# Turned spectrum copied from PSUM in runs of 8 by another grouping of the inverse rows; two W columns fetched over 128 partitions by the software queue; four A1 buffers

## Chip, cores, metric

One core of one Trainium2 chip. The metric is the device time of one execution in microseconds (us). The kernel before takes 497 us (median of its first three runs 496.99, from 496.23 to 497.87).

Names: PE is TensorE (PEld its weight loads), DVE is VectorE, ACT is ScalarE, POOL is GpSimd, SP is SyncE, whose queue issues most DMAs. "L455" is line 455 of the kernel at hand; the changed kernel's lines are a few off.

## The reference, cut to what matters

```python
x = A_x                                              # (1, 2048, 1024) bf16
g = sigmoid((x * gate_w).sum(-1, keepdims=True))
a = irfft2(rfft2(x) * (w_r + 1j * w_i))              # w_r, w_i: (2048, 513)
b = B(x)   # per channel p: h = Lam_bar[p] * h + Bu[t, p] over 2048 steps, then a product with C
return g * a + (1 - g) * b
```

This document is about `a`. The transform over 2048 rows is done in two steps of 128 and 16 with a "corner turn" between them: blocks go to DRAM (`turn1`, `turn2`) and come back with the rows in another order. Two columns of the spectrum, 0 and 512, need a correction of their own, so the kernel fetches columns 0 and 512 of W apart from the rest: about 2 x 2,048 places of 4 bytes, one row (1,026 bytes) apart.

## The kernel before: the parts in question

The first stage makes 16 blocks. Each is a product on PE (`fd`), a copy to SBUF on ACT (`X1`), a second product, a copy on DVE (`A1`) and a write to DRAM:

```python
for j in range(16):
    X1 = X1_next
    if j + 1 < 16: X1_next = fd(j + 1)            # PE L306, then the X1 copy on ACT, L309
    psa = psA.tile([P, 2, K], FP32, name="ps_s1", tag="ps")
    ... 4 matmuls, L318 to L321
    A1 = gta.tile([P, 2, K], BF16, name="A1")     # pool gta: 2 buffers
    nc.vector.tensor_copy(out=A1, in_=psa)        # L323
    nc.gpsimd.tensor_copy(out=Acol[:, j, :], in_=A1[:, :, 0])
    nc.sync.dma_start(out=turn1_dram[j], in_=A1)  # L325
```

In between, the two W columns are loaded on the SP queue; `Wp` is 128 partitions x 2 x 16 x 2:

```python
for ri, W in enumerate((A_w_r, A_w_i)):
    fl = ...                                      # the pair (W[s, 512], W[s+1, 0]) at row s
    nc.sync.dma_start(out=Wp[0:P - 1, ri], in_=fl[0:S - 16, 0:2].rearrange("(p b) k -> p b k", b=16))  # L586
    nc.sync.dma_start(out=Wp[P - 1:P, ri, 0:15], in_=...)                                              # L587
    ... two small ones, L588 and L589
Wc = ...                                          # three small copies on GpSimd, L591 to L593
# later, on VectorE:  Wc_f <- Wc                  # L357
```

The last step of the inverse is 16 blocks. Row m of 128 is split into m = 16a + b; block b holds the rows with that b, and its 8 rows (a = 0..7) for 16 values of q (output row 128q + m) go to ZT:

```python
t2_v = turn2_dram.rearrange("j (a b) c k -> b (j a) c k", a=8)
ZT_v = ZT.rearrange("p i q (a b) -> p b i q a", b=16)            # ZT: 128 x 8 x 16 x 128, bf16
for bp in range(16):
    Cq = fft["cq"].tile([P, 2, K], BF16, name="Cq")              # 6 buffers
    nc.sync.dma_start(out=Cq, in_=t2_v[bp])
    psz = psA.tile([P, 4, 2 * P], FP32, name="ps_is2", tag="ps") # 2 buffers
    ... 8 matmuls, L451 and L453
    nc.scalar.copy(out=ZT_v[:, bp], in_=psz.rearrange("p kc (c q a) -> p (kc c) q a", c=2, a=8))   # L455
```

PSUM is read in order; in ZT each element lands 16 elements (32 bytes) after the last. Then comes the long end: C GEMM (L512) and the column products with ZT (L530).

## Time and profile before

Three stretches matter. The middle stage, 119 to 216 us, is left out here: from the last turn1 write to the first Cq load it took 91.7 us.

| stretch | from, us | to, us | what holds it |
|---|---|---|---|
| first stage | 28 | 119 | in 47 to 78: the loads of W columns |
| last inverse step | 216 | 281 | ACT, copies to ZT |
| C GEMM and the rest | 281 | 495 | PE |

The page of the kernel before: the span in 40 slices of 12.4 us; a digit is the busy share in tenths, PEclk the granted clock of TensorE, DMA the busy share of the 16 DMA engines.

```profile
PE   4797306989979777554444699999999999999994
DVE  3863005893989899999000006579999999985131
ACT  3599003633246555379999912222122212110010
PEclk9789656999989999965555599999999999999999
DMA  8999012213418998862210202200120130001001
```

Slices 5 and 6 (49.5 to 74.3 us) show 3 and 0 on PE and 0 on DVE and ACT. In slices 19 to 23 ACT shows 9s, and PE mostly 4s at a granted clock of 0.5. After that PE is full.

The chain that ended last, in order of time (start us, us, what):

```profile
47.33 12.27 SPq L587
...
61.34 12.04 SPq L325
...
74.77 1.84 DMA Wf<-in_A_w_i_dram
76.99 1.23 DVE A_662 L323
78.27 0.59 PE ps_s_677 L318
...
215.77 64.80 ACT ZT L455 x15
280.62 1.03 PE ps_y L512 x2
```

The chain runs through two holds of the SP queue of 12 us each, then through a wait for W, into A1 and PE. Later it is 65 us of nothing but ZT copies.

Who waited for whom (us in total, times, longest), of the kernel before:

```profile
POOL Wc L592 <- DMA Wp<-in_A_w_i_dram: 33.0, 1, 33.0
...
DVE Wc_f L357 <- POOL Wc L593: 26.9, 1, 26.9
PE ps_s_677 L318 <- DVE A_662 L323: 23.6, 1, 23.6
```

On VectorE's track L357, which needs the W columns, stands in front of the A1 copy; it began at 76.88 us and the copy at 76.99. So late columns stop A1, and A1 stops PE.

Busy time in chosen stretches (start:end, length, then busy us of PE, PEld, DVE, ACT, POOL, then granted clock, DMA share, GB/s), kernel before:

```profile
47.00:78.00 31.00, 5.03 (x17) 2.28 (x16) 2.34 (x3) 3.41 (x7) 0.70 (x4) 0.60 0.15 28
78.00:119.00 41.00, 37.08 (x173) 21.46 (x177) 30.70 (x42) 21.27 (x25) 6.68 (x13) 0.93 0.21 77
211.00:281.00 70.00, 34.71 (x152) 21.50 (x152) 24.41 (x37) 67.13 (x18) 0.00 (x0) 0.52 0.24 70
281.00:487.00 206.00, 204.78 (x1294) 123.66 (x1313) 145.36 (x213) 43.12 (x38) 0.00 (x0) 0.99 0.12 43
```

In 31 us from 47 on, no engine works more than 5.03 us. From 281 to 487 PE works 204.78 of 206 us: whatever is gained earlier shifts this part, and it can't shrink by itself.

### The profile page before, as it was taken

To read this page: it belongs to the slowest core of one execution; us is meant where nothing else is said; L and a number is where in the kernel's file an instruction comes from. 1 tells how busy PE (TensorE), PEld (TensorE's weight loads), DVE (VectorE), ACT (ScalarE), POOL (GpSimd) and SP (SyncE) were. 2 spreads that over 40 slices of the span, in tenths; PEclk is the share of its full clock that TensorE was granted. 3 is DMA by queue.
4 is the path that set the end of the run, shared out by engine and by line. 5 is a ranking of instruction groups with operands and counts; after the bars stand their busy time and mean duration, and the time that the engine had idled before them with its cause. 6 is when DMAs were issued, how large, how long until landed. Compare 5 with 4: busy or idle time off the path is not lost.

```text
span 495.2 us, 6444 instructions
## 1 busy us (share of the span) xinstructions
PE 391.8 (79%) x2568; PEld 244.5 (49%) x2601; DVE 314.5 (64%) x532; ACT 211.6 (43%) x195; POOL 18.3 (4%) x42
## 2 busy tenths in 40 slices
PE   4797306989979777554444699999999999999994
PEld 4674103556845444333223246676576567654442
DVE  3863005893989899999000006579999999985131
ACT  3599003633246555379999912222122212110010
POOL 0000001120003100100000000000000000000000
PEclk9789656999989999965555599999999999999999
DMA  8999012213418998862210202200120130001001
GB/s 309 258 212 162 1 12 73 85 66 107 109 42 244 244 230 261 192 191 64 64 42 1 85 1 85 86 1 0 66 85 23 65 106 23 1 22 44 21 23 42
DMA packets 60991, 46.37 MB, mean 94 GB/s; under 512 B 42658, under 2 KB 47138, under 8 KB 60578
## 3 DMA queue, kind: packets, MB, share of 16 engines
q1 hardware_dynamic: 60882, 45.95, 34.2%
q8 instruction: 20, 0.33, 0.3%
q14 instruction: 9, 0.07, 0.0%
q10 hardware_dynamic: 80, 0.01, 0.0%
HBM read 22.87 MB, written 14.69 MB: 76 GB/s over the span
## 4 chain that ended last, share of the span: by engine, by line
PE 54%; ACT 21%; SPq 8%; DVE 6%; DMA 6%; issue 3%; POOL 1%; ACTq 0%; POOLq 0%; another core or an unknown queue 0%; DVEq 0%
PE ps_y L512 23%; PE psu L258 14%; ACT ZT L455 13%; PE ps_id L530 6%; PE ps_fd L306 4%; SPq L587 3%; SPq L325 3%; DMA Bb<-turn_scratch 2%; PE pt L551 2%; DVE u L277 2%; PE ps_y L516 1%; SPq L503 1%; DMA vec_97<-in_B_Dskip_dram 1%; DMA W_b<-in_A_w_r_dram 1%; DMA Cq<-turn_scratch 1%
## 5 line engine op out<-in xcount | busy, mean ns | idle before, releaser
L512 PE MATMUL ps_y<-CT_981,h 128*128 128x512 bf16 x252 | 96.8, 384 | 2.6 <-ACT ZT L455 2.0
L512 PE MATMUL ps_y<-CT_982,h 128*128 128x512 bf16 x244 | 93.8, 384 | 0.4 <-issue 0.2
L512 PEld LDWEIGHTS <-h 128*128 128x128 bf16 x512 | 49.8, 99 | 58.5 <-issue 3.0
L277 DVE TENSOR_TENSOR_SCAN u<-r_sb,carry,u 128x256 bf16<-128x256 f32 x112 | 74.6, 730 | 0.0
L288 DVE TENSOR_TENSOR h<-u,tab 128x2048 bf16<-128x2048 bf16 x16 | 19.5, 1217 | 64.9 <-DMA y_scratch<-ye 64.9
L533 ACT ACTIVATE eo<-ps_id,gB 128x1024 bf16<-128x1024 f32 x16 | 17.8, 1113 | 99.1 <-PE ps_id L530 99.1
L260 ACT CAST u<-psu 128x1024 bf16<-128x1024 f32 x32 | 32.2, 1012 | 60.9 <-PE psu L258 47.0
L306 PE MATMUL ps_fd<-G_sb,preT 128*128 128x512 bf16 x125 | 31.9, 397 | 3.9 <-ACT X_813 L309 0.5
L530 PE MATMUL ps_id<-Gi_sb,ZT 128*128 128x512 bf16 x124 | 29.4, 379 | 0.2
L269 DVE TENSOR_TENSOR su<-u,tab 128x2048 bf16<-128x2048 bf16 x16 | 19.6, 1222 | 15.4 <-ACT u L260 15.0
L453 PEld LDWEIGHTS <-Cq 128*128 128x128 bf16 x64 | 8.8, 138 | 39.0 <-issue 35.9
L535 DVE TENSOR_TENSOR ga<-eo 128x512 bf16<-128x512 bf16 x16 | 6.7, 418 | 31.3 <-ACT eo L533 31.3
L306 PEld LDWEIGHTS <-preT 128*128 128x128 bf16 x128 | 18.7, 146 | 14.1 <-issue 7.1
L258 PE MATMUL psu<-xT,BT_118 128*128 128x256 bf16 x128 | 17.9, 288 | 5.5 <-ACT u L260 5.5
L270 DVE TENSOR_TENSOR u<-u,tab 128x2048 bf16<-128x2048 bf16 x16 | 19.6, 1223 | 0.4
L287 DVE TENSOR_TENSOR sg<-u,tab 128x2048 bf16<-128x2048 bf16 x16 | 19.5, 1218 | 0.1
L318 PE MATMUL ps_s_677<-X_655,T_sb 128*128 128x512 bf16 x1 | 0.6, 586 | 23.6 <-DVE A_662 L323 23.6
L530 PEld LDWEIGHTS <-ZT 128*128 128x128 bf16 x128 | 12.0, 98 | 12.3
L258 PE MATMUL psu<-xT,BT_114 128*128 128x256 bf16 x128 | 17.8, 283 | 0.1
L258 PE MATMUL psu<-xT,BT_119 128*128 128x256 bf16 x128 | 17.6, 280 | 0.0
L258 PEld LDWEIGHTS <-BT_118 128*128 128x128 bf16 x128 | 13.2, 103 | 8.7 <-issue 5.7
L258 PE MATMUL psu<-xT,BT_117 128*128 128x256 bf16 x128 | 17.5, 280 | 0.0
(608 smaller groups left out, 758.9 us busy)
## 6 DMA issues: line engine op xcount, KB each, us to landing
Bb<-turn_scratch SPq DMA_DIRECT2D x16, 256.0 KB, 3.7
Cq<-turn_scratch SPq DMA_DIRECT2D x16, 256.0 KB, 2.9
out_dram<-ga SPq DMA_DIRECT2D x16, 256.0 KB, 2.0
W_b<-in_A_w_r_dram SPq DMA_DIRECT2D x16, 128.0 KB, 3.5
W_b<-in_A_w_i_dram SPq DMA_DIRECT2D x16, 128.0 KB, 3.2
y_scratch<-ye SPq DMA_DIRECT2D x4, 512.0 KB, 3.3
yl<-y_scratch SPq DMA_DIRECT2D x4, 512.0 KB, 3.4
T_sb<-c_T SPq DMA_DIRECT2D x1, 1152.0 KB
```

The source lines that it names most:

```text
L258: nc.tensor.matmul(psu[:, j, ri, :], lhsT=BT[jb][:, ri, d8, :], rhs=xT[:, d8, TC * c:TC * (c + 1)], start=(d8 == 0), stop=(d8 == 7))
L260: nc.scalar.copy(out=u[:, 2 * j2:2 * j2 + 2], in_=psu)
L269: nc.vector.tensor_mul(out=su, in0=u[:, :, ::-1, :], in1=bc(1))
L270: nc.vector.tensor_mul(out=u, in0=u, in1=bc(0))
L277: nc.vector.tensor_tensor_scan(out=u[:, j, ri, :], data0=rb, data1=u[:, j, ri, :], initial=(0.0 if c == 0 else carry[:, jb, ri:ri + 1]), o ...
L287: nc.vector.tensor_mul(out=sg, in0=u[:, :, ::-1, :], in1=bc(3))
L288: nc.vector.tensor_mul(out=h, in0=u, in1=bc(2))
L306: nc.tensor.matmul(ps[:, cls, :], lhsT=preT_A[:, cls, d4, j, :], rhs=G_sb[:, cls, d4, :], start=(d4 == 0), stop=(d4 == 3))
L455: nc.scalar.copy(out=ZT_v[:, bp], in_=psz.rearrange("p kc (c q a) -> p (kc c) q a", c=2, a=8))
L512: nc.tensor.matmul(psy[:, 512 * dh:512 * (dh + 1)], lhsT=hs[c, jb // 4][:, jb % 4, ri, P * tq:P * (tq + 1)], rhs=CT[ri][:, jb, 512 * dh:51 ...
L530: nc.tensor.matmul(pse[:, cls, :], lhsT=fft["ZT"][:, 4 * cls + i, tb, :], rhs=fft["Gi"][:, 4 * cls + i, :], start=(i == 0), stop=(i == 3))
L533: nc.scalar.activation(out=eo, in_=pse, func=ACT.Copy, scale=gB[:, tb:tb + 1])
```

## The change

Its intent: copies to ZT with fewer scattered writes; W columns out of SP's way; and more A1 buffers, so that a late consumer of A1 doesn't stop PE.

```diff
-            A1 = gta.tile([P, 2, K], BF16, name="A1")
+            A1 = gta.tile([P, 2, K], BF16, name="A1", bufs=4)
 ...
-        t2_v = turn2_dram.rearrange("j (a b) c k -> b (j a) c k", a=8)
-        ZT_v = ZT.rearrange("p i q (a b) -> p b i q a", b=16)
-            nc.sync.dma_start(out=Cq, in_=t2_v[bp])
+            nc.sync.dma_start(out=Cq, in_=turn2_dram[:, 8 * bp:8 * bp + 8])
 ...
-            nc.scalar.copy(out=ZT_v[:, bp], in_=psz.rearrange("p kc (c q a) -> p (kc c) q a", c=2, a=8))
+            nc.scalar.copy(out=ZT[:, :, :, 8 * bp:8 * bp + 8],
+                           in_=psz.rearrange("p kc (c q a) -> p (kc c) q a", c=2, a=8))
 ...
-                nc.sync.dma_start(out=Wp[0:P - 1, ri], in_=fl[0:S - 16, 0:2].rearrange("(p b) k -> p b k", b=16))
-                nc.sync.dma_start(out=Wp[P - 1:P, ri, 0:15], in_=...)
-                ... two small ones, nc.sync
+                at = lambda b: bass.AP(W.tensor, ..., [[16 * (K + 1), P], [K + 1, 15], [1, 2]])
+                nc.gpsimd.dma_start(out=Wp[:, ri, 0:15], in_=at(0))
+                nc.gpsimd.dma_start(out=Wp[0:P - 16, ri, 15], in_=fl[15:16 * (P - 16):16, 0:2])
+                nc.gpsimd.dma_start(out=Wp[P - 16:P - 1, ri, 15], in_=...)
+                ... two small ones, nc.gpsimd
```

The rows are now split as m = 8b + a, so a block's 8 rows are neighbours in ZT (a run of 16 bytes) and in DRAM. Most of the W columns (15 of 16 places) now go in one transfer over all 128 partitions; the last place goes over 112 and 15.

More of the change, by code (lines that the diff above doesn't have):

```diff
@@ L526, in finish @@
     def finish(tb, psy=None):
+        ZT_t = fft["ZT"]
         pse = psU.tile([P, 2, K], FP32, name="ps_id", tag="psu")
@@ L529, in finish @@
             for i in range(4):
-                nc.tensor.matmul(pse[:, cls, :], lhsT=fft["ZT"][:, 4 * cls + i, tb, :], rhs=fft["Gi"][:, 4 * cls + i, :],
+                nc.tensor.matmul(pse[:, cls, :], lhsT=ZT_t[:, 4 * cls + i, tb, :], rhs=fft["Gi"][:, 4 * cls + i, :],
                                  start=(i == 0), stop=(i == 3))
@@ L585, in load_Wcols @@
                 fl = W.rearrange("s k -> (s k)")[K:K + (S - 1) * (K + 1)].rearrange("(s k) -> s k", k=K + 1)
-                nc.sync.dma_start(out=Wp[0:P - 1, ri], in_=fl[0:S - 16, 0:2].rearrange("(p b) k -> p b k", b=16))
-                nc.sync.dma_start(out=Wp[P - 1:P, ri, 0:15], in_=fl[S - 16:S - 1, 0:2].rearrange("(p b) k -> p b k", b=15))
-                nc.sync.dma_start(out=Wp[P - 1:P, ri, 15:16, 0:1], in_=W[S - 1:S, K:K + 1].unsqueeze(0))
-                nc.sync.dma_start(out=Wf[:, ri:ri + 1], in_=W.rearrange("(p b) k -> p b k", b=16)[:, 0, 0:1])
+                at = lambda b: bass.AP(W.tensor, W.offset + K + (K + 1) * b, [[16 * (K + 1), P], [K + 1, 15], [1, 2]])
+                nc.gpsimd.dma_start(out=Wp[:, ri, 0:15], in_=at(0))
+                nc.gpsimd.dma_start(out=Wp[0:P - 16, ri, 15], in_=fl[15:16 * (P - 16):16, 0:2])
+                nc.gpsimd.dma_start(out=Wp[P - 16:P - 1, ri, 15], in_=fl[16 * (P - 16) + 15:S - 1:16, 0:2])
+                nc.gpsimd.dma_start(out=Wp[P - 1:P, ri, 15:16, 0:1], in_=W[S - 1:S, K:K + 1].unsqueeze(0))
+                nc.gpsimd.dma_start(out=Wf[:, ri:ri + 1], in_=W.rearrange("(p b) k -> p b k", b=16)[:, 0, 0:1])
         Wc = fft["Wc"].rearrange("p b (c r) -> p r b c", r=2)
```

## The prediction

> **What bounds the kernel now.** From 281 to 487 us PE is busy about 99% at a granted clock of 0.96 to 1.00 (windows view); the change does not touch that. Two earlier stretches on the chain of waits are not PE-bound.
>
> (a) 47 to 78 us. The SP queue issues the two-column loads of W (lines 586 to 589). One issue holds the queue 12.27 us, and the turn1 write behind the second load 12.04 us. VectorE waits 26.9 us for the columns (Wc), GpSimd 33.0, PE 23.6 (waits view). In this window PE works 5.0 us, DVE 2.3, ACT 3.4. The DMA share is 0.10 with next to no bytes (windows, 62 to 73 us). [...]
>
> (b) 216 to 285 us. ACT copies the turned spectrum from PSUM to ZT: 16 copies of 128x1024, about 4.75 us each; 15 are 64.8 us of the chain. PE works half of the time, at half clock. Copies of the same size to contiguous rows (lines 260, 413, 434) take 1.01 us, the one writing every second element (line 309) 1.28. So the cost is the scattered write: one element every 32 bytes.
>
> **What the change does.**
> (b) ZT copies write runs of 8 elements (16 bytes): I estimate 1.05 to 1.3 us from the two neighbours. Cq loads keep their 256 KB; the first six ran at about 330 GB/s together (0.8 us each). PE needs about 1.7 us a block at half clock (trace), half of that warm. Pitch: 1.2 to 1.3 us instead of 4.3, the first two or three slower. The stage shrinks from 65 us to about 19: minus 46. C GEMM starts on a warm clock (it ran at half rate for 4.7 us): minus 2. VectorE has its units done at about 236 us, where GEMM would now begin.
>
> (a) The turn1 writes no longer stand behind W. About 4,000 descriptors at an estimated 11 ns of engine time each (share 0.10 over two times 14 us) are under 3 us over 16 engines. I expect the Pool instructions to be placed early, since Pool idles from 1.6 to 37 us. Four A1 buffers remove the 4.7 us wait of A1 for the first turn1 write and cover a late Acol copy. Expected: minus 25, at most 28.
>
> [...] If it lasts past 50 us, Acol and then A1 stall again: I allow 4 us.
>
> **Sum.** 497 - 46 - 2 - 25 + 4 = 428 us; 8 in 10 between 414 and 450. Faster by over 2%: 0.96, within 2%: 0.02, slower: 0.02.
>
> **What would show it.** ZT copies near 1.1 us; C GEMM starting 15 to 20 us after the first ZT copy; from there to the end still about 214 us. No 12 us SP issues; PE idle before line 318 under 5 us instead of 23.6; DVE not waiting for Wc; turn1 writes every 3.3 us or so from 46 us on.
>
> **What would make it wrong.** 16-byte runs still cost several us; [...] the columns land late and block VectorE where it reads Wc; small descriptors slow the x loads, which fill the DMA in the first 28 us.

In (a), that one DMA engine carried the old load was my assumption; the share of 0.10 is the time of about 1.6 of 16 engines (an estimate, 0.10 x 16), and the estimate of under 3 us takes it that the new load uses all 16. "It" in "If it lasts past 50 us" is the time for which issuing the W loads keeps GpSimd busy. The trace before could not show it, so the 4 us are an allowance and rest on no measurement.

## The result

The changed kernel takes 417.94 us (median of 4 runs, 415.64 to 418.23), against 497.41 us (4 runs) before. The ratio of the fast runs is 0.8395, 95% interval 0.8361 to 0.8429. Ratios here are the mean time of one kernel's fast runs over that of the other's fast runs of the same rounds, so they differ a little from the ratio of the quoted medians. Executions over 1.5% slower than the fastest of the same kernel are left out of the means. The prediction was 428 us, 414 to 450.

The page of the changed kernel; a slice is 10.4 us:

```profile
PE   2699998999797869749999999999999999999993
DVE  2985669839898988999707739999999999863211
ACT  1789983332275646428512220412213212111111
PEclk9989999999899998959999999999999999999999
DMA  7999922244069998797402110022012100000010
```

Both holes are gone. What is left of the low PE slices is the first one and parts of the middle stage.

The chain of the changed kernel:

```profile
62.52 1.90 PE ps_fd L306 x8
64.50 1.33 ACT X_835 L309
65.87 1.90 PE ps_fd L306 x8
...
88.26 2.02 DMA turn_scratch<-A_971
...
180.24 4.06 DMA Cq<-turn_scratch
...
203.66 3.60 PE ps_y L511 x16
```

The first stage now alternates between PE and the X1 copy, a block every 3.35 us, without a hole. C GEMM starts at 203.7 instead of 280.6 us.

One and the same ZT copy, the twelfth of 16, before (L455) and after (L453), as min, median and max ns:

```profile
L455 ACT CAST ZT<-ps_is_2196 x1: 4747/4747/4747, 262.9 to 262.9; 128x1024 bf16<-128x1024 f32 x1
L453 ACT CAST ZT<-ps_is_2198 x1: 1014/1014/1014, 199.2 to 199.2; 128x1024 bf16<-128x1024 f32 x1
```

GpSimd's own track of the changed kernel (start us, us, engine, line, operation), with its first W transfer and its last small copy of the columns:

```profile
1.53 1.38 POOL L587 DMA_DIRECT2D Wp<-in_A_w_r_dram  x1
...
16.10 1.25 POOL L595 COPY Wc<-Wf 128x2 bf16<-128x2 bf16 x1
```

The columns are complete 17.4 us into the span, and L357 converts them at 22.2 us without a wait. Issuing 1,920 places (L587) took GpSimd 1.38 us. In the list of waits of the changed kernel neither a line with L357 nor one with L318 appears among the longest 37; what GpSimd still waits for the columns is:

```profile
POOL Wc L594 <- DMA Wp<-in_A_w_i_dram: 3.1, 1, 3.1
```

The stretches of the changed kernel that answer to those above:

```profile
48.00:90.00 42.00, 38.26 (x201) 23.50 (x200) 31.70 (x42) 23.44 (x30) 6.57 (x13) 1.00 0.30 109
181.00:204.00 23.00, 21.30 (x153) 16.08 (x153) 22.66 (x33) 16.65 (x18) 0.00 (x0) 0.82 0.69 190
204.00:410.00 206.00, 205.46 (x1321) 123.59 (x1318) 146.87 (x218) 40.24 (x39) 0.00 (x0) 1.00 0.13 45
```

The last line is the control: the same PE-bound work, 206 us before and after.

A tally by landmarks of the two traces (us):

| landmark | before | after | gained so far |
|---|---|---|---|
| fourth block's L318 | 50.02 | 46.81 | 3.2 |
| fifth block's L318 | 78.27 | 50.13 | 28.1 |
| last turn1 write issued | 118.83 | 88.26 | 30.6 |
| first Cq load issued | 210.51 | 180.24 | 30.3 |
| first ZT copy | 215.77 | 186.39 | 29.4 |
| C GEMM starts | 280.62 | 203.66 | 77.0 |
| end of span | 495.2 | 416.4 | 78.8 |

So in these two traces the W part gave about 30 us, the ZT part 48 to 49.

### The profile page after: what moved, and what is told of

The parts are those of the page before. It is cut to its first block, busy times and chain, and to the rows that moved or that the text cites. A ratio compares the mean times of both kernels' runs of the same rounds, so it can differ in the third digit from the quotient of the medians.

```text
span 416.4 us, 6481 instructions
## 1 busy us (share of the span) xinstructions
PE 372.7 (89%) x2601; PEld 236.1 (57%) x2601; DVE 314.5 (76%) x532; ACT 157.7 (38%) x195; POOL 26.8 (6%) x52
## 4 chain that ended last, share of the span: by engine, by line
PE 66%; ACT 11%; DVE 10%; DMA 6%; issue 3%; SPq 2%; POOL 0%; ACTq 0%; POOLq 0%; DVEq 0%
PE ps_y L511 27%; PE psu L258 17%; PE ps_id L530 7%; PE ps_fd L306 4%; DVE u L277 2%; DMA W_b<-in_A_w_r_dram 2%; PE ps_y L515 2%; SPq L502 2%; DMA Bb<-turn_scratch 1%; DMA vec_97<-in_gate_w_dram 1%; DMA Cq<-turn_scratch 1%; DVE xT L552 1%; PE pt L551 1%; ACT cs_f L192 1%; DVE preT L558 1%
## 5 line engine op out<-in xcount | busy, mean ns | idle before, releaser
L511 PE MATMUL ps_y<-CT_983,h 128*128 128x512 bf16 x256 | 97.0, 379 | 0.0
L511 PE MATMUL ps_y<-CT_984,h 128*128 128x512 bf16 x256 | 97.0, 379 | 0.0
L306 PE MATMUL ps_fd<-G_sb,preT 128*128 128x512 bf16 x128 | 30.2, 379 | 4.0 <-ACT X_815 L309 0.5
L258 PE MATMUL psu<-xT,BT_118 128*128 128x256 bf16 x128 | 17.2, 282 | 5.5 <-ACT u L260 5.5
L258 PE MATMUL psu<-xT,BT_114 128*128 128x256 bf16 x128 | 17.9, 285 | 0.0
L258 PE MATMUL psu<-xT,BT_115 128*128 128x256 bf16 x128 | 16.9, 273 | 0.0
L258 PE MATMUL psu<-xT,BT_117 128*128 128x256 bf16 x128 | 16.7, 273 | 0.0
L258 PE MATMUL psu<-xT,BT_119 128*128 128x256 bf16 x128 | 16.7, 272 | 0.0
L258 PE MATMUL psu<-xT,BT_116 128*128 128x256 bf16 x128 | 16.1, 273 | 0.0
```

The costliest lines, as they stand in the source:

```text
L258: nc.tensor.matmul(psu[:, j, ri, :], lhsT=BT[jb][:, ri, d8, :], rhs=xT[:, d8, TC * c:TC * (c + 1)], start=(d8 == 0), stop=(d8 == 7))
L306: nc.tensor.matmul(ps[:, cls, :], lhsT=preT_A[:, cls, d4, j, :], rhs=G_sb[:, cls, d4, :], start=(d4 == 0), stop=(d4 == 3))
L511: nc.tensor.matmul(psy[:, 512 * dh:512 * (dh + 1)], lhsT=hs[c, jb // 4][:, jb % 4, ri, P * tq:P * (tq + 1)], rhs=CT[ri][:, jb, 512 * dh:51 ...
```

## The experiments

Twelve kernels ran. "Before" and the experiment were timed on the same chip in the same rounds. The order of instructions was compared between the builds, leaving out names and line numbers: PE and ACT have the same order in all of `before`, `after`, e1 to e5; DVE differs only in the place of L357. So differences of these runs are differences of waiting, not of schedule, except for L357.

| run | what | median us | ratio to before | 95% interval |
|---|---|---|---|---|
| e1 | ZT part alone | 448.03 | 0.9031 | 0.9002 to 0.9059 |
| e2 | W part alone, 2 A1 buffers | 475.08 | 0.9574 | 0.9531 to 0.9616 |
| e3 | W part and 4 A1 buffers | 468.89 | 0.9456 | 0.9412 to 0.9499 |
| e4 | 4 A1 buffers alone | 497.48 | 1.0018 | 0.9977 to 1.0058 |
| e5 | after, W pieces on SP | 421.72 | 0.8501 | 0.8448 to 0.8554 |
| e6 | after, W over 127 partitions on GpSimd | 495.57 | 0.9897 | 0.9810 to 0.9985 |
| e7 | after, Cq by the old rows | 417.79 | 0.8416 | 0.8373 to 0.8460 |
| e8, e12 | write patterns, one look each | 437.83, 452.80 | - | - |
| e9 | after, again | 419.92 | 0.8431 | 0.8406 to 0.8457 |
| e10 | e3 again | 468.88 | 0.9412 | 0.9379 to 0.9445 |
| e11 | after, X1 copy turned too | 415.99 | 0.8362 | 0.8334 to 0.8391 |

### e1: the ZT part alone

```diff
 (kernel before, with only the new Cq load and the new ZT copy)
```

> The kernel before with only the regrouped inverse rows (ZT copies in runs of 8). Theory: the two parts of the change lie in two separate stretches of the chain, so they add. The ZT part alone should bring 48 to 49 us: 497.4 - 48.5 = about 449 us, with ZT copies of 1.01 us and the 23.6 us PE wait before line 318 unchanged. Rival: part of the gain needs the other part (warm clock, other DMA traffic); then this run and the W-and-buffers run together fall short of 79.5 us by more than 3 us.

Measured: 448.03 us, 48.1 us less than before (0.0969 x 496.3). As expected.

### e2, e3, e4: the W part, with and without the buffers

```diff
 (e2: kernel before, with only the new W loads)
 (e3: e2, and)
-            A1 = gta.tile([P, 2, K], BF16, name="A1")
+            A1 = gta.tile([P, 2, K], BF16, name="A1", bufs=4)
 (e4: kernel before, with only this line)
```

> The kernel before with only the W loads on GpSimd's queue over 128 partitions, A1 still in 2 buffers. Theory: the first turn1 write stands behind the B transposes in SP's queue until about 48 us, so with 2 buffers the third A1 copy waits until about 50 us instead of running at 44.5: about 6 us of the 30 us remain, time near 473 us. Rival: the buffers do nothing once W is out of the queue; then 467 us, like the run with both.

> The kernel before with the W loads on GpSimd's queue and 4 A1 buffers, ZT copies as before. Theory: 30 to 31 us less than before, about 467 us, and ZT copies still 4.75 us. Together with the ZT-only run the gains should add up to the 79.5 us of the whole change within 2 us. Rival (parts interact): the sum is off by more than 3 us.

> The kernel before with only 4 A1 buffers. Theory: the stall is not a shortage of A1 buffers: VectorE stands at the conversion of the W columns (line 357) until they land at about 77 us, so only the 4.7 us wait of the third A1 copy can go, and time falls by 0 to 4 us (493 to 497). Rival: the stall is A1 running out behind the held turn1 writes; then 4 buffers let PE go on for two more blocks of 3.3 us each and time falls by 7 to 10 us (487 to 490).

Measured: e2 475.08 us, e3 468.89, e4 497.48. VectorE's track of e2, the third A1 copy, and in brackets what it waited for:

```profile
50.53 1.23 DVE L323 CAST A<-ps_s 128x1024 bf16<-128x1024 f32 x1 [6.01 <-DMA turn_scratch<-A]
```

In e2 the third copy waits 6.01 us for the first turn1 write, which SP issues only after the last B transpose, at 47.9 us. Four buffers remove this: e3 is 6.2 us faster than e2. Without the W part the buffers give nothing, because VectorE stands at L357. VectorE's track of e4:

```profile
77.30 0.20 DVE L357 CAST Wc_f<-Wc 128x64 f32<-128x64 bf16 x1 [30.82 <-POOL Wc L593]
```

In e4 the third A1 copy did run 3.5 us earlier (45.25 us against 48.74 before), and the wait at L357 grew by 3.9 us, to 30.82. A wait that was removed came back as a longer wait for the W columns. (497.48 us is half a us above the range that I expected, and the same as before.) So the stall was the W data, not the number of A1 buffers; the buffers are worth 6 us only once W is out of the way.

One thing did not fit: by the ratios the gains of e1 and e3 (48.1 + 27.0 us) fell 4.6 us short of the whole change, more than the 3 us that I had named as the sign of an interaction. This is taken up in e9 and e10.

### e5, e6: which half of the W change does it, the queue or the spread?

```diff
 (e5: kernel after, with)
-                nc.gpsimd.dma_start(out=Wp[:, ri, 0:15], in_=at(0))      (and the four others)
+                nc.sync.dma_start(out=Wp[:, ri, 0:15], in_=at(0))
 (e6: kernel after, with the old 127 partitions)
-                nc.gpsimd.dma_start(out=Wp[:, ri, 0:15], in_=at(0))
+                for b0 in range(0, 16, 4):
+                    nc.gpsimd.dma_start(out=Wp[0:P - 1, ri, b0:b0 + 4], in_=...[:, b0:b0 + 4])
```

In e6 each piece is also cut into four; no run has the uncut piece on this queue. So e6 differs from the changed kernel in the cut as well as in the partitions.

> The changed kernel with its new W pieces (128, 112 and 15 partitions) issued from the SP queue instead of GpSimd's. Theory A: the 12 us holds came from one engine taking 2,032 tiny descriptors; over 16 engines an issue is short, so SP loses only the 10 issues (about 5 us) at its place behind the B transposes, the columns land by about 56 us, VectorE waits a few us: 418 to 426 us. Theory B: many tiny descriptors hold the SP queue however they are spread; then issues of several us remain and the time is 435 us or more.

> The changed kernel with the old 127-partition pieces on GpSimd's queue (each cut into 4[...]). Theory A: the queue and the early place are what count; the columns are then 10 to 20 us later than the 16 us of the changed kernel, and VectorE, which reads them at 22 us in its order, waits 5 to 15 us early on: 420 to 433 us. Theory B: over the software queue 127 partitions are spread over all engines too[...]: nothing changes, 416 to 420 us, landing times like those of the changed kernel (5 to 9 us).

Measured: e5 421.72 us, e6 495.57. In e5 the same pieces over 128 and 112 partitions hold SP for a moment only (SP's track):

```profile
44.42 0.43 SPq L587 DMA_DIRECT2D Wp<-in_A_w_r_dram  x1
44.90 0.93 SPq L588 DMA_DIRECT2D Wp<-in_A_w_r_dram  x1
45.87 2.08 SPq L589 DMA_DIRECT2D Wp<-in_A_w_r_dram  x1
```

Theory A's time (418 to 426 us) and its short issues hold for SP's queue. The packets in the traces show the difference directly. Before, packets of at most 4 bytes leave at a steady 170 per us through both holds, at which 2,032 of them take 12.0 us, the length of a hold; in e5 they reach 979 per us, and the columns of both loads are at GpSimd at 53.0 us, 8.6 us after the first issue. That the slow rate is that of one engine was not shown: the DMA share was 0.10 of 16 engines (62 to 73 us), the time of about 1.6 (an estimate, 0.10 x 16). With the new pieces, the software queue is worth about 4 us more: 0.8501 against 0.8416 for e7 (its Cq loads alone differ from the changed kernel), or 3.5 to 5.3 us against the changed kernel's 0.8431 and 0.8395. They were run at other times. The intervals of e5 and e7 overlap, so the size is uncertain.

With the software queue and 127 partitions, on the other hand, nearly the whole gain of both parts is lost. GpSimd's track of e6:

```profile
31.22 4.54 POOL L587 DMA_DIRECT2D Wp<-in_A_w_r_dram  x1 [6.64 <-issue]
...
105.20 0.26 POOL L594 COPY Wc<-Wp 128x30 bf16<-128x30 bf16 x1 [7.41 <-DMA Wp<-in_A_w_i_dram]
```

and its waits:

```profile
DVE Wc_f L357 <- POOL Wc L595: 79.5, 1, 79.5
```

This was my largest miss: I expected 416 to 433 us under either theory. Issuing one piece of 508 places took GpSimd 4.54 us, against 1.38 us for 1,920 places over 128 partitions, GpSimd also stood idle between the issues (39.2 us in front of the pieces), and the pieces took 9.8 to 32.1 us from issue to landing. The columns were complete at 105 us. L357 stands early in VectorE's order here, as in the changed kernel, in front of copies of x: it cost 79.5 us. The profiled run of e6, 501.41 us, counts as slow (2.4% above the fastest, 489.54; the ratio in the table uses the fast two of four runs); no point here rests on a difference of that size. Also, SP's B transposes took longer in e6 (the first one held SP 15.5 us, 6.4 us before); whether the software queue's packets did that, these runs do not settle.

And e6 did not do what it was built for: the trace does not show its pieces on one engine. The software queue's packets, megabytes and share of the 16 engines' time, first in the changed kernel, then in e6:

```profile
q0 software_dynamic: 352, 0.02, 0.7%
...
q0 software_dynamic: 1344, 0.26, 4.2%
```

The eight pieces hold 0.016 MB (8 x 2,032 bytes), and e6 moved 16 times that. Sorted by size, its large packets are 896 of 256 bytes and 128 of 240, which is 8 x 16 sets of 2,032 bytes, so by the trace's packets each piece was carried 16 times over. The DMA share was 1.28 to 1.48 from 30 to 60 us (packets can overlap, so it passes 1), against 0.10 in the hole before. The trace does not name the engines, and why it happened stays open. So e6 shows that this form is costly on the software queue, and not that the number of partitions is what makes it so. The same pieces over 128 partitions, cut into four, were not run.

### e7: is it the write, or the load?

```diff
 (kernel after, with)
-            nc.sync.dma_start(out=Cq, in_=turn2_dram[:, 8 * bp:8 * bp + 8])
+            nc.sync.dma_start(out=Cq, in_=t2_v[bp])                        (wrong result on purpose)
```

> The changed kernel, but Cq loaded by the old row pattern (128 rows 32 KB apart instead of 16 blocks of 8 neighbouring rows); the result is wrong on purpose, the timing is meant. Theory: the gain is all in the write to ZT; the load pattern decides only the landing of Cq (3.8 us median with the new rows against 2.9 before), so this run is 0 to 1 us faster than the changed kernel. Rival: the new load pattern is part of the gain; then this run is over 2 us slower.

Measured: 417.79 us, ratio 0.8416: the same as the changed kernel (0.8395 and 0.8431). The load pattern is no part of the gain. Its own small loss, a first ZT copy 0.9 us later in the landmarks above, is below what these timings resolve.

### e8, e12: what about the write is slow?

After each ZT copy, one more copy of a 128x1024 block, each with another pattern. Both were meant to give a wrong result. e12 did; e8 stayed within the tolerance, so a pass of that comparison says little about single blocks of ZT.

```diff
 (kernel after, inside the loop over bp; scr is ZT as one row of 16,384, flat is psz as one row)
+            if bp == 0: nc.scalar.copy(out=scr[:, 0:1024], in_=flat)
+            elif bp == 4: nc.scalar.copy(out=<every 16th element of scr>, in_=flat)
+            ...
```

> The changed kernel with one extra copy of the same 128x1024 PSUM block to SBUF after each ZT copy, each with another write pattern (wrong result on purpose; read the durations only). Theory A (ScalarE pays about 4.2 us per 1,024 writes that each fall into a 32-byte granule of their own): step of 2 elements 1.28 us, 4 elements (8 bytes) 1.3 to 1.6, 8 elements (16 bytes) about 2.2, 16 elements (32 bytes) 4.75; runs of 2 at 64-byte pitch about 2.2, runs of 4 at 128-byte pitch 1.0 to 1.3, runs of 8 1.01. Theory B (only writes below 4 contiguous bytes are slow): runs of 2 already 1.0 us and steps of 2 to 16 elements all alike. Reading PSUM in steps of 16 elements with a contiguous write: 1.0 us in both. VectorE: contiguous 1.22 us; with the step of 16 elements either the same (the cost is ScalarE's alone) or over 3 us (the cost is SBUF's).

> A second set of extra copies of a 128x1024 block (read durations only). The first set: single 2-byte writes cost 1.30, 2.44, 4.72 and 4.50 us at steps of 4, 8, 16 and 32 bytes, while runs of 2 elements at a 64-byte pitch cost 1.01 us, and VectorE pays 4.43 us at 32 bytes too. Theory C (a write of less than 4 bytes is what costs): 4-byte elements at steps of 8 and 32 bytes take 1.0 us; 2-byte elements at odd steps (3, 5, 7, 9, 15) are slow like their neighbours, growing from about 2 us to 4.7; runs of 2 that straddle two 4-byte words are slow again, over 2 us. Theory D[...]: odd steps are fast, 1.0 to 1.3 us, and 4-byte elements at a 32-byte step slow. From SBUF instead of PSUM, step 16: as slow on ScalarE and VectorE if the write is the cause.

Groups of instructions of e8 (line, engine, operation, shapes, count, busy us, mean ns):

```profile
L466 ACT CAST ZT<-ps_is 128x1024 bf16<-128x1024 f32 x1 | 4.7, 4724 | 0.0
L468 ACT CAST ZT<-ps_is 128x1024 bf16<-128x1024 f32 x1 | 4.5, 4495 | 0.0
L464 ACT CAST ZT<-ps_is 128x1024 bf16<-128x1024 f32 x1 | 2.4, 2442 | 0.0
L462 ACT CAST ZT<-ps_is 128x1024 bf16<-128x1024 f32 x1 | 1.3, 1304 | 0.0
...
L470 ACT CAST ZT<-ps_is 128x1024 bf16<-128x1024 f32 x1 | 1.0, 1009 | 0.0
```

L462, 464, 466 and 468 write single elements at steps of 4, 8, 16 and 32 bytes; L470 writes runs of two elements (4 bytes) every 64 bytes. Groups of e12:

```profile
L482 ACT CAST ZT<-ps_is 128x1024 bf16<-128x1024 f32 x1 | 2.4, 2395 | 0.0
...
L462 ACT COPY ZT<-ps_is 128x1024 f32<-128x1024 f32 x1 | 2.0, 2010 | 0.0
...
L464 ACT COPY ZT<-ps_is 128x1024 f32<-128x1024 f32 x1 | 1.1, 1091 | 0.0
```

L482 writes runs of two that straddle two 4-byte words; L462 and L464 write 4-byte elements at steps of 32 and 8 bytes.

All results together, ACT from PSUM, 1,024 elements per partition:

| what is written | step or pitch, bytes | us |
|---|---|---|
| contiguous | 2 | 1.01 |
| single 2-byte elements | 4, 6, 8, 10, 12, 14 | 1.30, 1.87, 2.44, 3.03, 3.56, 4.13 |
| single 2-byte elements | 16, 18, 24, 30, 32 | 4.72, 4.64, 4.65, 4.51, 4.50 |
| 4-byte elements | 8, 32 | 1.09, 2.01 |
| aligned runs of 2, 4, 8 (2-byte) | 64, 128, 256 | 1.01, 1.02, 1.02 |
| straddling runs of 2 | 64 | 2.40 |
| contiguous, PSUM read in steps of 64 bytes | - | 1.01 |

Theory A (a fixed cost per 32-byte place) falls: runs of two at a 64-byte pitch touch 512 such places and cost nothing extra. Theory B (all steps alike) falls on the growth from 1.30 to 4.72. Theory D (power-of-two steps) falls on steps of 18 and 30 bytes, as slow as 16 and 32. Theory C (less than 4 bytes is what costs) holds for the straddling runs, but 4-byte elements at 32 bytes still took 2.01 us, not 1.0. What describes all of it: the time is about the number of 16-byte stretches of SBUF touched times 4.5 ns if 4-byte words in them are written in part, or times 2 ns if only whole 4-byte words are written, and never under 1.0 us. (The 16 is read off the table, which is flat, 4.50 to 4.72 us, from a step of 16 bytes on.) For a step of 8 bytes: 512 stretches x 4.5 = 2.3 (2.44 measured); of 16 bytes or more: 1,024 x 4.5 = 4.6 (4.50 to 4.72); 4-byte elements at 32 bytes: 1,024 x 2 = 2.0 (2.01); runs of 2 at 64 bytes: 512 x 2 = 1.0 (1.01). This is a description fitted to single instructions, not a shown mechanism. It is not ACT's alone: VectorE took 4.43 us from PSUM at a step of 32 bytes and 1.23 contiguous, GpSimd 4.51 and 1.04 from SBUF, ACT from SBUF 4.49. VectorE from SBUF took 2.32 us, once; that stays unexplained.

So, by these single copies, runs of 8 were more than was needed: an aligned run of 2 took 1.01 us at a pitch of 64 bytes and 1.13 at 32. No kernel with shorter runs was timed.

### e9, e10: do the two parts add?

```diff
 (e9: kernel after, unaltered; e10: e3, unaltered)
```

> The changed kernel, unaltered, run again on the chip of the next two. It gives the base for both. Expected: ratio to before 0.838 to 0.842, about 417 us.

> The W loads and 4 A1 buffers again (first time 27.0 us less than before; with the 48.1 us of the ZT part alone that is 4.6 us short of the whole change). All engines but the ZT copies and Cq loads run the same instructions in the same order as the changed kernel, so up to the first Cq load the two can differ by scatter only. Theory (no interaction, scatter of the first run): the difference to the changed kernel of this call is 48 to 50 us, that is about 466 us. Rival (an interaction): the difference stays at 51 us or more, 468 us and up.

Measured: e9 419.92 us, 0.8431; e10 468.88 us, 0.9412. The ratio of e9 is just outside what I expected, and e10's time alone is where the rival had it (468 us and up), because both ran slower. The difference, which is what the two theories disagree on, is 49.0 us: the ZT part gives with the W part what it gives without (48.1). The W part is 29.3 us here (0.0588 x 497.9), 27.0 in e3. No interaction shows; the 4.6 us were most likely scatter.

### e11: the same lesson on the X1 copy

The table pointed at another copy: L309 writes single elements at every second place, on the chain.

```diff
-            nc.scalar.copy(out=X1.rearrange("p r (i c) -> p c r i", c=2), in_=ps.rearrange("p c (r i) -> p c r i", r=2))
+            nc.scalar.copy(out=X1.rearrange("p r (i c) -> p r i c", c=2), in_=ps.rearrange("p c (r i) -> p r i c", r=2))
```

> The changed kernel with the X1 copy (line 309) turned the same way as ZT: the same elements, but written to SBUF contiguously while PSUM is read in steps; it wrote single 2-byte elements at every second place (1.28 to 1.32 us). The pattern run showed 1.01 us for a stepped read with a contiguous write. In the first stage PE (1.90 us) and this copy (1.31 us) alternate on the chain, 16 blocks at 3.35 us. Theory: X1 copies 1.01 us, blocks 3.05 us, time 4 to 5 us less than the changed kernel of this call. Rival: PE, 90% busy there, has other work in the gap[...]; then less than 1.5 us.

Measured: 415.99 us, correct, ratio 0.8362 against 0.8431 for the changed kernel: 3.9 us by the medians, 3.4 by the ratios. The X1 copies (min, median, max ns) of e9:

```profile
L309 ACT CAST X<-ps_fd x16: 1277/1304/1316, 34.7 to 86.3; 128x1024 bf16<-128x1024 f32 x16
```

and of e11:

```profile
L309 ACT CAST X<-ps_fd x16: 985/1012/1013, 32.6 to 82.1; 128x1024 bf16<-128x1024 f32 x16
```

The copies fell to 1.01 us as expected, and most blocks follow each other after 3.04 us instead of 3.35. Two blocks around 70 to 77 us take 3.9 and 3.5 us, and there the chain runs through VectorE (A1 copies and scans) instead, so a little less than the expected 4 to 5 us came out. It is 0.8%, but the two intervals do not overlap. It is the fastest version.

## Why the prediction was right, point by point

- **Right: two stretches off PE, and a PE-bound end that only shifts.** C GEMM to the end took 214.6 us before and 212.7 after (214 was predicted).
- **Right: the ZT part.** Predicted minus 46 and minus 2; e1 measured 48.1 us, e9 against e10 49.0. The copies took 1.01 us (1.05 to 1.3 predicted), and C GEMM started 17.3 us after the first ZT copy (15 to 20). The warm clock came as said: the matmuls of 256 columns followed each other after 0.21 us in the first 4.7 us of the stretch (184.3 to 189.0) and after 0.11 us from then on. The granted clock was 0.50 in those 4.7 us and 0.99 from 189 to 204 us.
- **Right in direction, too narrow in its reason: "one element every 32 bytes".** e8 and e12 show that the spacing is half of it; the other half is whether whole 4-byte words are written (at a step of 32 bytes 4-byte elements took 2.01 us, 2-byte elements 4.50).
- **Right: 127 partitions were the trouble of the W loads.** e5 shows it: same queue, same places, other partition counts, 979 packets per us instead of 170, and no 12 us holds. That 127 partitions mean one engine was my assumption and was not shown, neither by the share of 0.10 (about 1.6 of 16 engines) nor on the software queue (e6). The prediction put more weight on SP's queue than it deserved: of about 30 us the software queue accounts for about 4.
- **The mis-sized term: "minus 25, at most 28", and "I allow 4 us".** The sum had 21 us for the W part; it measured 27.0 (e3) and 29.3 (e10), and 30.3 to 30.6 in the landmarks. The landmarks show where: 3.2 us of A1's wait for the first turn1 write, 24.9 us of hole, and 2.4 us after the hole, where the clock was 0.93 before and 1.00 now (that the clock is the reason is argued, not tested). I had the last one for C GEMM and forgot it here. The 4 us for GpSimd's issuing were not needed: 1.38 and 1.24 us for the two large transfers, 17.4 us until the columns were usable. All ten W issues were out by 10.7 us, the two large ones by 6.3 us, while VectorE stood idle from 1.7 to 8.5 us; so this run hardly tests whether VectorE's work delays such issues. (In e6 a piece took 4.54 to 4.73 us whether VectorE worked or waited, so this was not the cause there.) The undershoot of the W part is 6 to 8 of the 10 us between 428 and 418, by e3 and e10; the rest was not traced.
- **Half right: "small descriptors slow the x loads".** SP's B transposes ended later and the first turn1 write went out at 48.27 instead of 45.98 us (in e5, without early W loads, at 44.00). The x loads themselves were not compared. Four A1 buffers took that up; with two it cost 6.0 us (e2).

## What to carry to other kernels

When a copy writes SBUF in steps, turn the steps to the reading side or regroup the data until at least two neighbouring 2-byte elements on a 4-byte boundary are written together (1.01 us against 4.50 to 4.72 for a block of this size here); look for copies whose time exceeds that of a contiguous copy of the same size. For a load of many small pieces, look at the partition count before the queue: here 128 and 112 instead of 127 brought about 26 of the 30 us on the same queue (e5). And compare the bytes that a queue moved with the bytes that you asked for; in e6 they differ 16-fold. And before counting on more buffers, look at what stands in front of the consumer in its engine's order: four buffers were worth nothing while VectorE stood at another wait, and 6 us once it was gone.
